# Cached attention for one token per sequence on one core: order of the last loads, and order of the tail on VectorE, TensorE and ScalarE

## The chip, the core and the metric

The kernel runs on one core of one Trainium2 chip. The core has TensorE (PE in the profile; PEld is its weight load), VectorE (DVE), ScalarE (ACT), GpSimd (POOL) and SyncE (SP), which here issues the loads. 16 DMA engines move the data. The metric is the device time of one execution in microseconds; the number compared is the median over several executions.

## What is computed

One decoding step of grouped attention over the last 512 positions of a cache: 32 sequences ("batches"), 32 query heads, 8 K/V heads, head size 128, all bf16.

```python
B, Sq, D = 32, 1, 512
Hq, Hkv, Sk, Dh = 32, 8, 2048, 128
W = min(4096, max(256, Sk // 4))                 # 512
q = (x @ wq).reshape(B, Sq, Hq, Dh).transpose(0, 2, 1, 3)
k = repeat(k_cache[:, :, Sk - W:, :], 4, axis=1)
v = repeat(v_cache[:, :, Sk - W:, :], 4, axis=1)
p = softmax(einsum("bhqd,bhkd->bhqk", q, k) * Dh ** -0.5)
o = einsum("bhqk,bhkd->bhqd", p, v)
out = o.transpose(0, 2, 1, 3).reshape(B, Sq, Hq * Dh) @ wo
```

K and V of the window are 32 MB each (in units of 1024 KB), `wq` and `wo` 4 MB each.

## The kernel before

Each engine has a program of its own, written out by hand; engines meet at semaphores. Nothing reorders the instructions of an engine: what stands first runs first, and a wait holds back all that is behind it on that engine.

The work goes by quads, four batches each, eight in all. K comes in 16 chunks of 2 MB, two for a quad. Three K buffers rotate, so chunk n may be issued only when chunk n-3 has been transposed (the wait on `pe_T[3]` in `load_k`). V comes by batch, two transfers of 0.5 MB for each, into eight rotating buffers: batch b may be issued only when batch b-8 has been multiplied (the wait on `pe_PV` in `load_v`). All these loads stand in one order on SP: chunk n, then the V of batches 2n-4 and 2n-3; after the last chunk the four remaining batches; then `wo` in eight pieces, into two of the K buffers; at the very end the store of the result.

A step v of the main loop (32 steps, four to a quad) does on TensorE:

- `transposes(v)`: half a K chunk, 32 blocks of 128x128, into four PSUM banks (`KT_ps`). DVE empties three of these (line 366), ACT the fourth (line 455).
- at the first step of a quad, `scores` of the quad before (line 258), into `S_ps`
- `pv_matmuls(v - 7)`: V of one batch times the transposed probabilities `PT_sb`, 32 matmuls (line 291), into `QO_ps`. This bank is single: batch b waits until DVE has copied batch b-1 out (`ot_evac`, line 403).
- at the third step of a quad, `pt_transposes` of the quad before (line 273): P, expanded by DVE to `P_ex`, is transposed into `PT_ps`, and ACT copies it to `PT_sb` in two halves (`pt_evac`, line 474). The batches of that quad wait for both halves.

Between scores and P transposes lies the softmax of a quad: DVE takes the maximum (372) and scales it (374), ACT takes the exponential (463), DVE the reciprocal (380), and four instructions of DVE, `p_expand`, write the probabilities into `P_ex` (389), one for each 32 partitions.

After the loop comes the tail: scores of the last quad, batches 25 to 27, P transposes of the last quad, `select` for batches 0 to 27 (line 303: 16 matmuls with the 0/1 matrix `band`, which arrange the heads for the output product; they write the two first banks of `KT_ps`, and DVE and ACT copy one half each to `o_sel`, lines 429 and 489), batches 28 to 31, `select` for these (303, copied at 433), the product with `wo` (340), copies (436, 496) and the store (167).

In the tail of before DVE runs: maximum, scaling, reciprocal, four expansions, then the copies of batches 25, 26, 27, the copy of the selection, and the copies of batches 28 to 31. ACT runs: exponential, the two halves of `pt_evac`, its half of the selection, and at the end its half of the output.

Of the kernel before, what the change touches and what calls it, by code (L numbers as in the profile page):

```python
# [12 lines left out]
def bass_standalone__sliding_block_cached__sampling_kernel(  # L13
# [7 lines left out]
):  # L21
    B, Sq, D = x.shape
    _, HKV, SK, DH = k_cache.shape
    HD = wq.shape[1]
    HQ = HD // DH
# [14 lines left out]
    NQUAD = B // 4  # L40
    NVB = 4 * NQUAD
    PVLAG = 7
    NCH = 2 * NQUAD
# [5 lines left out]
    SELCUT = 28  # L49

    with ExitStack() as es:
# [75 lines left out]
        def cache_rows(cache, b, h):  # L127
            return cache[b, 4 * h:4 * h + 4, SK - W:, :].rearrange("g (s r) d -> s g (r d)", s=NS)

        @block.sync  # L130
        def _(sp):
            for kt in range(1, DKT):
                sp.dma_start(wq_sb[:, kt, :], wq[kt * P:(kt + 1) * P, :]).then_inc(sem_wq[kt], 16)  # L133

            def load_k(n):
                q, e = divmod(n, 2)
                if n >= NK:
                    sp.wait_ge(pe_T[3], 2 * (n - NK) + 2)
                rows = k_cache[4 * q:4 * q + 4, :, SK - W:, :].rearrange("b g (s r) d -> (b g) s (r d)", s=KS)
                sp.dma_start(  # L140
                    K_sb[:, n % NK].rearrange("p r d -> p (r d)"), rows[:, :, e * CR * DH:(e + 1) * CR * DH]
                ).then_inc(sem_k[n % NK], 16)

            def load_v(b):
                if b >= NV:
                    sp.wait_ge(pe_PV, b - NV + 1)
                for h in range(2):
                    sp.dma_start(  # L148
                        V_sb[:, b % NV, h].rearrange("p r d -> p (r d)"), cache_rows(v_cache, b, h)
                    ).then_inc(sem_v[b % NV], 16)  # L150

            for n in range(NCH):
                load_k(n)
                if n >= 2:
                    load_v(2 * n - 4)
                    load_v(2 * n - 3)
            for b in range(B - 4, B):
                load_v(b)
            for hg in range(NHG):
                sp.wait_ge(pe_T[3], NVB - 4 + 2 * (hg // 4))  # L160
                sp.dma_start(
                    wo_sb[:, hg].rearrange("p i n -> p (i n)"),
                    wo[hg * 512:(hg + 1) * 512, :].rearrange("(m i) n -> m (i n)", i=4),
                ).then_inc(sem_wo[hg], 16)
            sp.wait_ge(dve_out, 2)
            sp.wait_ge(act_out, 2)
            sp.dma_start(
                out.rearrange("b s n -> b (s n)"), out_sb[:, :, :].rearrange("b c n -> b (c n)")
            ).then_inc(sem_out, 16)
            sp.wait_ge(sem_out, 16)  # L170
# [35 lines left out]
        def _(pe):  # L206
# [59 lines left out]
            def pt_transposes(q):  # L266
                pe.wait_ge(dve_P, 4 * q + 4)
                pe.wait_ge(act_PT, 2 * q)
                if q == 0:
                    pe.wait_ge(dve_qt, 1)  # L270
                    pe.wait_ge(act_qt, 1)
                for r in range(NR):
                    ins = pe.matmul(  # L273
                        PT_ps[:, r // 8, (r % 8) * 128:(r % 8 + 1) * 128],
                        lhsT=P_ex[:, r, :, :].rearrange("p s g -> p (s g)"),
                        rhs=ident[:, :],
                        start=True, stop=True, is_transpose=True, tile_position=(0, 0),
                    )
                    if r % 8 == 7:
                        ins.then_inc(pe_PT, 1)  # L280
# [39 lines left out]
            scores(NQUAD - 1)  # L320
            for b in range(NVB - PVLAG, SELCUT):
                pv_matmuls(b)
            pt_transposes(NQUAD - 1)
            pe.wait_ge(pool_band, 2)
            pe.wait_ge(dve_T, 3 * NVB)
            pe.wait_ge(act_T, NVB)
            nb = SELCUT
            select(0, nb, lambda i: KT_ps[:, i // 2, :].bitcast(F32)[
                :, (i % 2) * NHG * nb:(i % 2 + 1) * NHG * nb])
            for b in range(SELCUT, B):  # L330
                pv_matmuls(b)
            nl = B - SELCUT
# [16 lines left out]
        @block.vector  # L349
        def _(dve):  # L350
            dve.wait_ge(pe_xT, 1)
            dve.tensor_copy(
                xT_sb[:, :, :], S_ps[:, 0:DKT * 32].rearrange("p (kt b) -> p kt b", b=32)
            ).then_inc(dve_xT, 1)
            dve.wait_ge(pe_qt, 1)
            dve.tensor_copy(
                QT_sb[:, 0:16, :].rearrange("p h b -> p (h b)"), PT_ps[:, 0, :].bitcast(F32)
            ).then_inc(dve_qt, 1)

            def kt_evac(v, t):  # L360
                q = v // 4
                if v % 4 == 0 and t == 0 and q >= 2:
                    dve.wait_ge(pe_S, q - 1)
                dve.wait_ge(pe_T[t], v + 1)
                r0 = 32 * (v % 4) + 8 * t
                dve.tensor_copy(  # L366
                    KT[q % 2][:, r0:r0 + 8].rearrange("p r a s -> p (r a s)"), KT_ps[:, t, :]
                ).then_inc(dve_T, 1)

            def softmax_a(q):  # L370
                dve.wait_ge(pe_S, q + 1)
                dve.tensor_reduce(maxv[:, q:q + 1], S_ps[:, :], AX.X, ALU.max).then_inc(dve_sm, 1)  # L372
                dve.wait_ge(dve_sm, 2 * q + 1)
                dve.tensor_scalar(  # L374
                    negmax[:, q:q + 1], maxv[:, q:q + 1], -SCALE, None, op0=ALU.mult
                ).then_inc(dve_sm, 1)

            def softmax_b(q):
                dve.wait_ge(act_exp, q + 1)
                dve.reciprocal(recip[:, q:q + 1], sums[:, q:q + 1]).then_inc(dve_sm2, 1)  # L380
                dve.wait_ge(dve_sm2, q + 1)
                if q == 0:
                    dve.wait_ge(pool_ex, 1)
                else:
                    dve.wait_ge(pe_PT, 2 * q)

            def p_expand(q, c):
                rows = slice(32 * c, 32 * c + 32)
                dve.tensor_scalar(  # L389
                    P_ex[rows, :, :, c], P_f32[rows, :].rearrange("p (r s) -> p r s", r=NR),  # L390
                    recip[rows, q:q + 1], None, op0=ALU.mult,
                ).then_inc(dve_P, 1)

            def sel_evac(bank, i0, ni, b0, b1):
                return (
                    o_sel[:, i0:i0 + ni, :, b0:b1],
                    KT_ps[:, bank, :].bitcast(F32)[:, 0:ni * NHG * (b1 - b0)].rearrange(
                        "p (i g b) -> p i g b", i=ni, g=NHG),
                )

            def ot_evac(b):
                dve.wait_ge(pe_PV, b + 1)
                dve.tensor_copy(oT_sb[:, :, b], QO_ps[:, 0:HQ]).then_inc(dve_oT, 1)  # L403

            for v in range(NVB):
                q, k = divmod(v, 4)
                kt_evac(v, 0)
                if k == 1 and q >= 1:
                    softmax_b(q - 1)
                    p_expand(q - 1, 0)  # L410
                kt_evac(v, 1)
                if k == 1 and q >= 1:
                    p_expand(q - 1, 1)
                kt_evac(v, 2)
                if k == 1 and q >= 1:
                    p_expand(q - 1, 2)
                    p_expand(q - 1, 3)
                if k == 0 and q >= 1:
                    softmax_a(q - 1)
                if v >= PVLAG:  # L420
                    ot_evac(v - PVLAG)
            softmax_a(NQUAD - 1)
            softmax_b(NQUAD - 1)
            for c in range(G4):
                p_expand(NQUAD - 1, c)
            for b in range(NVB - PVLAG, SELCUT):
                ot_evac(b)
            dve.wait_ge(pe_sel, 1)
            dve.tensor_copy(*sel_evac(0, 0, 2, 0, SELCUT)).then_inc(dve_sel, 1)
            for b in range(SELCUT, B):  # L430
                ot_evac(b)
            dve.wait_ge(pe_sel, 2)
            dve.tensor_copy(*sel_evac(3, 0, 4, SELCUT, B)).then_inc(dve_sel, 1)
            dve.wait_ge(pe_fin, 1)
            for c in range(2):
                dve.tensor_copy(
                    out_sb[:, c, :], KT_ps[32 * c:32 * (c + 1), 2, :].bitcast(F32)[:, 0:128]
                ).then_inc(dve_out, 1)

        @block.scalar  # L440
        def _(act):
# [37 lines left out]
            for v in range(NVB):  # L479
# [4 lines left out]
                if k == 2 and q >= 1:  # L484
                    pt_evac(q - 1)
            do_exp(NQUAD - 1)
            pt_evac(NQUAD - 1)
            act.wait_ge(pe_sel, 1)
            act.activation(
                o_sel[:, 2:4, :, 0:SELCUT],  # L490
                KT_ps[:, 1, :].bitcast(F32)[:, 0:2 * NHG * SELCUT].rearrange("p (i g b) -> p i g b", i=2, g=NHG),
                ACTF.Copy,
            ).then_inc(act_sel, 1)
            act.wait_ge(pe_fin, 1)
            for c in range(2, 4):
                act.activation(
# [30 lines left out]
```

## Time and profile before

| what | value |
|---|---|
| median of 8 runs | 198.55 us (197.2 to 198.89) |
| the profiled execution | 197.96 us |
| its span | 196.2 us |
| PE busy | 139.6 us (71%) |
| DVE busy | 104.6 us (53%) |
| ACT busy | 57.5 us (29%) |
| mean granted TensorE clock | 0.896 |
| DMA | 75.95 MB, mean 387 GB/s |
| K chunk, issue to landing | 22.2 us (median) |
| V transfer, issue to landing | 20.6 us (median) |

The span runs from the first to the last instruction of the profiled execution. In a row of the timeline the first number is the start in microseconds, the second the length, then engine, line, operation, tile written and tile read, shape, and xcount, the number of instructions merged into the row. A bracket at the end tells how long the engine stood idle before and what released it. "SPq" rows are issues of transfers, not their landing. Where pipelined instructions overlap, a row can begin a little before the end of the one above.

### The profile page before, as it was taken

To read this page: it belongs to the slowest core of one execution; us is meant where nothing else is said; L and a number is where in the kernel's file an instruction comes from. 1 tells how busy PE (TensorE), PEld (TensorE's weight loads), DVE (VectorE), ACT (ScalarE), POOL (GpSimd) and SP (SyncE) were. 2 spreads that over 40 slices of the span, in tenths; PEclk is the share of its full clock that TensorE was granted. 3 is DMA by queue.
4 is the path that set the end of the run, shared out by engine and by line. 5 is a ranking of instruction groups with operands and counts; after the bars stand their busy time and mean duration, and the time that the engine had idled before them with its cause. 6 is when DMAs were issued, how large, how long until landed. Compare 5 with 4: busy or idle time off the path is not lost.

```text
span 196.2 us, 5984 instructions
## 1 busy us (share of the span) xinstructions
PE 139.6 (71%) x2724; PEld 119.1 (61%) x2724; DVE 104.6 (53%) x190; ACT 57.5 (29%) x70; POOL 11.9 (6%) x43
## 2 busy tenths in 40 slices
PE   0440989395896689677949598849884988808874
PEld 0330976294776667665749568745874588507774
DVE  0000694964469535963595349833983398472211
ACT  3000262315132622362115223522352234311301
POOL 8302000100010001000100010000000000000000
PEclk9999999969699969997888879997999699995857
DMA  5999999999999999999999999999999999999600
GB/s 202 426 451 421 428 398 440 395 427 410 435 400 430 405 419 419 413 421 412 412 413 432 408 431 407 423 413 423 403 421 413 425 402 406 407 410 406 255 17 7
DMA packets 13369, 75.95 MB, mean 387 GB/s; under 512 B 1504, under 2 KB 1568, under 8 KB 10784
## 3 DMA queue, kind: packets, MB, share of 16 engines
q1 hardware_dynamic: 13296, 75.54, 93.8%
q8 instruction: 21, 0.34, 0.7%
q10 hardware_dynamic: 48, 0.03, 0.1%
q14 instruction: 4, 0.03, 0.0%
HBM read 75.53 MB, written 0.03 MB: 385 GB/s over the span
## 4 chain that ended last, share of the span: by engine, by line
DMA 43%; PE 27%; SPq 14%; DVE 11%; issue 2%; ACT 1%; DVEq 0%
DMA K_sb<-in_k_cache_dram 43%; SPq L148 12%; PE KT_ps L241 11%; DVE P_ex L389 6%; PE QO_ps L291 6%; PE S_ps L258 6%; DVE w_sb L366 2%; PE KT_ps L340 2%; PE KT_ps L303 2%; DVE oT_sb L403 1%; PE PT_ps L273 1%; SPq L133 1%; SPq L140 1%; ACT w_sb L455 1%; ACT P_f L463 0%
## 5 line engine op out<-in xcount | busy, mean ns | idle before, releaser
L241 PE MATMUL KT_ps<-ident,K_sb 128*128 128x128 bf16 x1024 | 72.5, 238 | 31.7 <-DMA K_sb<-in_k_cache_dram 31.7
L241 PEld LDWEIGHTS KT_ps<-ident,K_sb 128*128 128x128 bf16 x1024 | 67.0, 107 | 34.1 <-DMA K_sb<-in_k_cache_dram 33.3
L366 DVE COPY KT_sb<-KT_ps 128x1024 bf16<-128x1024 bf16 x48 | 31.3, 688 | 18.9 <-PE KT_ps L241 18.6
L366 DVE COPY w_sb<-KT_ps 128x1024 bf16<-128x1024 bf16 x48 | 31.4, 688 | 14.9 <-PE KT_ps L241 14.7
L291 PE MATMUL QO_ps<-PT_sb,V_sb 128*128 128x16 bf16 x1024 | 30.9, 171 | 11.0 <-DVE oT_sb L403 10.7
L291 PEld LDWEIGHTS QO_ps<-PT_sb,V_sb 128*128 128x128 bf16 x1024 | 28.4, 97 | 16.5 <-DVE oT_sb L403 12.1
L455 ACT ACTIVATE KT_sb<-KT_ps 128x1024 bf16<-128x1024 bf16 x16 | 16.4, 1024 | 41.3 <-PE KT_ps L241 41.3
L455 ACT ACTIVATE w_sb<-KT_ps 128x1024 bf16<-128x1024 bf16 x16 | 16.4, 1025 | 35.5 <-PE KT_ps L241 35.5
L389 DVE TENSOR_SCALAR P_ex<-P_f,recip 32x512 bf16<-32x512 f32 x32 | 25.3, 792 | 1.3 <-DVE recip L380 0.3
L474 ACT ACTIVATE PT_sb<-PT_ps 128x1024 bf16<-128x1024 bf16 x16 | 15.5, 1021 | 14.3 <-PE PT_ps L273 14.3
L372 DVE TENSOR_REDUCE maxv<-S_ps 128x1 f32<-128x512 f32 x8 | 5.5, 691 | 21.8 <-PE S_ps L258 21.8
L403 DVE CAST oT_sb<-QO_ps 128x32 bf16<-128x32 f32 x32 | 9.5, 296 | 9.0 <-PE QO_ps L291 8.8
L203 POOL COPY QBD<-QT_sb 128x32 bf16<-128x32 bf16 x32 | 6.0, 232 | 124.8 <-PE S_ps L258 116.4
L463 ACT ACTIVATE P_f<-S_ps,negmax 128x512 f32<-128x512 f32 x8 | 5.5, 687 | 22.0 <-DVE negmax L374 22.0
L258 PE MATMUL S_ps<-w_sb,QBD 128*32 128x512 bf16 x128 | 11.2, 504 | 0.5 <-ACT w_sb L455 0.5
L258 PE MATMUL S_ps<-KT_sb,QBD 128*32 128x512 bf16 x128 | 11.2, 502 | 0.0
L273 PE MATMUL PT_ps<-ident,P_ex 128*128 128x128 bf16 x128 | 9.3, 232 | 0.0
L221 PE MATMUL PT_ps<-xT_sb,w_sb 128*128 128x32 bf16 x128 | 4.1, 188 | 6.4 <-DMA w_sb<-in_wq_dram 6.4
L273 PEld LDWEIGHTS PT_ps<-ident,P_ex 128*128 128x128 bf16 x128 | 8.1, 104 | 0.0
L221 PEld LDWEIGHTS PT_ps<-xT_sb,w_sb 128*128 128x128 bf16 x128 | 3.7, 104 | 6.8 <-DMA w_sb<-in_wq_dram 4.6
L258 PEld LDWEIGHTS S_ps<-w_sb,QBD 128*32 128x32 bf16 x128 | 3.7, 113 | 6.2 <-issue 6.2
L258 PEld LDWEIGHTS S_ps<-KT_sb,QBD 128*32 128x32 bf16 x128 | 3.6, 113 | 5.7 <-issue 5.6
(30 smaller groups left out, 29.3 us busy)
## 6 DMA issues: line engine op xcount, KB each, us to landing
K_sb<-in_k_cache_dram SPq DMA_DIRECT2D x16, 2048.0 KB, 22.2
V_sb<-in_v_cache_dram SPq DMA_DIRECT2D x64, 512.0 KB, 20.6
w_sb<-in_wq_dram SPq DMA_DIRECT2D x4, 1024.0 KB, 8.2
K_sb<-in_wo_dram SPq DMA_DIRECT2D x8, 512.0 KB, 15.0
x_sb<-in_x_dram ACTq DMA_DIRECT2D x1, 32.0 KB, 2.7
out_dram<-out_sb SPq DMA_DIRECT2D x1, 32.0 KB, 1.5
```

Source lines behind the costliest of these rows:

```text
L148: sp.dma_start(V_sb[:, b % NV, h].rearrange("p r d -> p (r d)"), cache_rows(v_cache, b, h)).then_inc(sem_v[b % NV], 16)
L203: pool.tensor_copy(dst, src).then_inc(pool_qbd, 1)
L221: ins = pe.matmul(PT_ps[:, h // 16, :].bitcast(F32)[:, (h % 16) * 32:(h % 16 + 1) * 32], lhsT=wq_sb[:, kt, h * DH:(h + 1) * DH], rhs=xT_sb ...
L241: ins = pe.matmul(KT_ps[:, t, i * 128:(i + 1) * 128], lhsT=K_sb[:, n % NK, 32 * (v % 2) + 8 * t + i, :], rhs=ident[:, :], start=True, stop ...
L258: ins = pe.matmul(S_ps[32 * c:32 * c + 32, :], lhsT=QBD[:, (4 * q + j) % NQB, g, :], rhs=KT[q % 2][:, :, G * j + g, :], start=(j == 0 and ...
L273: ins = pe.matmul(PT_ps[:, r // 8, (r % 8) * 128:(r % 8 + 1) * 128], lhsT=P_ex[:, r, :, :].rearrange("p s g -> p (s g)"), rhs=ident[:, :], ...
L291: ins = pe.matmul(QO_ps[:, 16 * h:16 * h + 16], lhsT=V_sb[:, b % NV, h, r, :], rhs=PT_sb[:, q % 2, r, :].rearrange("p (c n) -> p c n", c=G ...
L366: dve.tensor_copy(KT[q % 2][:, r0:r0 + 8].rearrange("p r a s -> p (r a s)"), KT_ps[:, t, :]).then_inc(dve_T, 1)
L389: dve.tensor_scalar(P_ex[rows, :, :, c], P_f32[rows, :].rearrange("p (r s) -> p r s", r=NR), recip[rows, q:q + 1], None, op0=ALU.mult,).th ...
L403: dve.tensor_copy(oT_sb[:, :, b], QO_ps[:, 0:HQ]).then_inc(dve_oT, 1)
L455: act.activation(KT[q % 2][:, r0:r0 + 8].rearrange("p r a s -> p (r a s)"), KT_ps[:, 3, :], ACTF.Copy).then_inc(act_T, 1)
L474: act.activation(PT_sb[:, q % 2, 8 * i:8 * i + 8, :].rearrange("p r n -> p (r n)"), PT_ps[:, i, :], ACTF.Copy,).then_inc(act_PT, 1)
```

## The change

In the loads, the V batches that stood between K chunks 14 and 15 (24 and 25) and those that stood after chunk 15 (26 and 27) are all issued after chunk 15, ahead of 28 to 31. In the tail, DVE copies batch 25 out before the reciprocal and the copies of 26 and 27 between the expansions; TensorE does the selection of batches 0 to 27 before the last P transposes; and ACT copies its half of the selection before the two halves of `PT_sb`. The instructions are the same in kind and number.

```diff
             for n in range(NCH):
                 load_k(n)
-                if n >= 2:
+                if 2 <= n < NCH - 2:
                     load_v(2 * n - 4)
                     load_v(2 * n - 3)
-            for b in range(B - 4, B):
+            for b in range(B - 8, B):
                 load_v(b)
...
             scores(NQUAD - 1)
             for b in range(NVB - PVLAG, SELCUT):
                 pv_matmuls(b)
-            pt_transposes(NQUAD - 1)
             pe.wait_ge(pool_band, 2)
             pe.wait_ge(dve_T, 3 * NVB)
             pe.wait_ge(act_T, NVB)
             nb = SELCUT
             select(0, nb, lambda i: KT_ps[:, i // 2, :].bitcast(F32)[
                 :, (i % 2) * NHG * nb:(i % 2 + 1) * NHG * nb])
+            pt_transposes(NQUAD - 1)
             for b in range(SELCUT, B):
                 pv_matmuls(b)
...
             softmax_a(NQUAD - 1)
+            ot_evac(NVB - PVLAG)
             softmax_b(NQUAD - 1)
             for c in range(G4):
                 p_expand(NQUAD - 1, c)
-            for b in range(NVB - PVLAG, SELCUT):
-                ot_evac(b)
+                if NVB - PVLAG + 1 + c < SELCUT:
+                    ot_evac(NVB - PVLAG + 1 + c)
             dve.wait_ge(pe_sel, 1)
...
             do_exp(NQUAD - 1)
-            pt_evac(NQUAD - 1)
             act.wait_ge(pe_sel, 1)
             act.activation(
                 o_sel[:, 2:4, :, 0:SELCUT],
...
             ).then_inc(act_sel, 1)
+            pt_evac(NQUAD - 1)
             act.wait_ge(pe_fin, 1)
```

With `NVB = 32`, `PVLAG = 7`, `SELCUT = 28`, `NCH = 16` and `B = 32`, the loops above cover batches 25 to 27 before the cut and 28 to 31 after it.

## Prediction, made before the changed kernel had run

> **What bounds the kernel now.** I read the busy slices first, then the chain of waits, then the timeline of the last quads, then the granted clock by microsecond. The page says that transfers run without a pause almost to the end:
>
> ```profile
> DMA  5999999999999999999999999999999999999600
> DMA 43%; PE 27%; SPq 14%; DVE 11%; issue 2%; ACT 1%; DVEq 0%
> ```
>
> The second line is the chain that ended last, by engine. Up to the last quad it consists of K chunks and the queue that issues them; no compute engine sets the pace there. The timeline around the last two K chunks shows when they are issued (SPq), and what each issue stands behind:
>
> ```profile
> 128.88 1.02 SPq L140 DMA_DIRECT2D K_sb<-in_k_cache_dram  x1
> 129.94 9.01 SPq L148 DMA_DIRECT2D V_sb<-in_v_cache_dram  x4
> ...
> 137.59 1.95 PE L241 MATMUL KT_ps<-ident,K_sb 128*128 128x128 bf16 x32
> ...
> 139.57 0.54 SPq L140 DMA_DIRECT2D K_sb<-in_k_cache_dram  x1
> ```
>
> K chunk 14 goes out at 128.88 us, the four V transfers of batches 24 and 25 after it, chunk 15 at 139.57. Chunk 15 needs the buffer of chunk 12, which is free when the transposes of v=25 end: 137.59 + 1.95 = 139.54 us. So its issue is gated by TensorE, not by the V issues ahead of it. It lands 21.5 us later, where the next view shows PE waiting for it:
>
> ```profile
> 161.07 1.96 PE L241 MATMUL KT_ps<-ident,K_sb 128*128 128x128 bf16 x32 [0.84 <-DMA K_sb<-in_k_cache_dram]
> ...
> 163.47 0.30 DVE L403 CAST oT_sb<-QO_ps 128x32 bf16<-128x32 f32 x1
> 163.58 1.89 DVE L366 COPY w_sb<-KT_ps 128x1024 bf16<-128x1024 bf16 x3
> ...
> 163.82 0.96 PE L291 MATMUL QO_ps<-PT_sb,V_sb 128*128 128x16 bf16 x32 [0.79 <-DVE oT_sb L403]
> ```
>
> PE stood 0.84 us for chunk 15, transposed v=30, and then stood again, 0.79 us, for the evacuation of batch 22, which DVE reached only at 163.47 behind the four P expansions of quad 6. From the landing of chunk 14 (151.1) that DVE sequence is closed up. The tail, in the same timeline:
>
> ```profile
> 171.19 0.96 PE L291 MATMUL QO_ps<-PT_sb,V_sb 128*128 128x16 bf16 x32
> ...
> 172.02 0.15 DVE L374 TENSOR_SCALAR negmax<-maxv 128x1 f32<-128x1 f32 x1
> ...
> 173.47 3.24 DVE L389 TENSOR_SCALAR P_ex<-P_f,recip 32x512 bf16<-32x512 f32 x4 [0.29 <-DVE recip L380]
> 176.74 0.30 DVE L403 CAST oT_sb<-QO_ps 128x32 bf16<-128x32 f32 x1
> ...
> 177.10 1.02 PE L291 MATMUL QO_ps<-PT_sb,V_sb 128*128 128x16 bf16 x32 [4.95 <-DVE oT_sb L403]
> 178.16 0.30 DVE L403 CAST oT_sb<-QO_ps 128x32 bf16<-128x32 f32 x1 [1.12 <-PE QO_ps L291]
> ...
> 178.51 1.02 PE L291 MATMUL QO_ps<-PT_sb,V_sb 128*128 128x16 bf16 x32 [0.39 <-DVE oT_sb L403]
> ...
> 179.39 1.87 PE L273 MATMUL PT_ps<-ident,P_ex 128*128 128x128 bf16 x16
> ...
> 180.50 1.94 ACT L474 ACTIVATE PT_sb<-PT_ps 128x1024 bf16<-128x1024 bf16 x2 [7.51 <-PE PT_ps L273]
> ...
> 181.05 2.69 PE L303 MATMUL KT_ps<-oT_sb,band 128*128 128x224 bf16 x16
> ...
> 183.57 0.95 PE L291 MATMUL QO_ps<-PT_sb,V_sb 128*128 128x16 bf16 x32
> ```
>
> Batch 25 is multiplied by 172.15, but its evacuation waits until 176.74 behind softmax and four expansions; PE idles 4.95 us. Then batch 26, batch 27, the P transposes of quad 7, the selection and batch 28 follow each other. The clock and DMA share in single microseconds (PE busy, clock, DMA share, GB/s):
>
> ```profile
> 176.00:177.00 1.00, 0.00 (x0) 0.62 1.01 401
> 183.00:184.00 1.00, 1.00 (x24) 0.96 0.63 254
> 187.00:188.00 1.00, 0.61 (x23) 0.50 0.03 12
> ```
>
> The clock is half from about 176.25 (0.62 is the mean of 0.24 us full and 0.76 us half) to 183.07, and the last output weights land between 187 and 188 us.
>
> **Part 1, the loads.** Nothing is added or removed: K chunk 15 passes four V issues, so in order of the queue 2 MB stand behind it instead of ahead of it. At the 410 GB/s of the rows around 170 us, 4 x 0.52 MB are 5.1 us: chunk 15 lands at about 156 instead of 161. What SP must pass on the way: it now stands at the wait for v=25 from 129.9 to 139.57, and the V transfers of batches 24 and 25 go out from about 140 on, 10 us later than before. Behind them are V26 to V28, whose buffers are free by 148.4, and 11 issues between 139.57 and 149 at 0.54 to 0.7 us each (the shortest and the median V issue) take 6 to 8 us, so V29 (free at 157.6) and the output weights go out as before. This queue's transfers land about in the order of issue (chunks 14 and 15 went out 10.7 us apart and landed 10.0 apart), so batches 24 and 25 land at 161, where chunk 15 did; PE needs batch 24 at 167.34. Covered by 6 us; without that cover each us late would cost a us.
>
> The gain of Part 1 I take as zero. With chunk 15 there, v=30's transposes start at 160.25, when PE finishes batch 22, and end at 162.2 instead of 163.0. Next in PE's order is batch 23, and it waits for the cast at 163.47, which no part of this edit moves: 163.82 as before. The 0.84 us go into the second stall, 0.79 becoming about 1.6. Ends for the range: 0.84 us gained if that stall shrank too, and a loss taken up under the rivals.
>
> **Part 2, the casts among the expansions.** The same three casts of 0.30 us, placed earlier. Cast 25 at 172.20 (negmax ends 172.17; batch 25 is done) ends 172.50, ahead of the reciprocal at 173.02, which waits for the exponential anyway: free. PE starts batch 26 at 172.55 (a cast's end to the next matmul is 0.05 to 0.06) and ends at 173.55. Expansion 0 runs 173.47 to 174.25; cast 26 from 174.28 to 174.58; batch 27 from 174.63 to 175.6. Expansion 1 ends 175.4; cast 27 waits 0.25 for batch 27 and runs 175.63 to 175.95; expansions 2 and 3 end at 177.55, against 176.71. So the expansions end 0.84 us later and the casts of 25 to 27 are all out by 175.95 instead of 179.87.
>
> **Part 3, the selection ahead of the P transposes.** The selection starts at 176.0. In the trace it takes 2.52 us from its start to that of batch 28: 2.02 at half clock and 0.50 at full, so all at half clock 3.02 and all at full 1.51. I take the row as it is, as the clock's step can fall on either side. The P transposes start at 178.54 (expansions done at 177.55, no wait). From their start to ACT's first copy were 1.11 us, two copies 1.94: PT is ready at 181.59, batch 28 starts at 181.64. Before, PT was ready at 182.44, but PE was in the selection until 183.57: there the selection covered ACT's copies, and now nothing does. Between 181.64 and 183.57 lies the gain: **1.93 us**. ACT's selection copy (0.54) and DVE's (0.62) start at about 178.7 and end before the first PT half; they cost nothing. From batch 28 on every instruction is as before, 12.6 us to the end. The output weights are landed at 187.5 while the first is needed at 188.1 and the last at 191.2.
>
> Sum: 0 + 1.93 against a profiled execution of 197.96 us (span 196.2 and 1.8 around it), so 196.0 there. The median of the eight runs is 0.6 higher, 198.55: **196.6 us**.
>
> The trace shows the clock falling after 4 us of idle PE and rising after the closed-up transposes and selection. [...] By the page alone the selection could be anything from 1.5 to 3.0 us, the sum 195.3 to 197.1.
>
> **Rivals.**
> - *Full clock in the tail.* The stall of 4.95 us, in which the clock fell, is gone. Selection 1.51 (ends 177.5), transposes from 177.6, first copy 0.70 later as in quad 6 (164.64 weight load to 165.34 copy), copies 1.94: batch 28 at 180.3, gain 3.28, **195.3**. Against: batches 28 to 30, with the same pauses, ran from 183.07 at full clock and lost it again at 186.5.
> - *Chunk 15 counts.* The 0.84 us of its wait come on top: **195.8**. Against: the second stall, and the chain, which passes through chunk 14 and the expansions.
> - *Clock falls one step sooner.* Half clock from 169 on: scores 3.18 us (as at 153.58) instead of 2.46, two batches 0.06 each, selection 3.02: 1.43 - 0.72 - 0.12 = 0.6 gained, **198.0**, no change. For it: scores did run so at 153.58; against: here PE is busy up to the scores.
> - *The queue runs thin (slower).* SP issues nothing for 9.6 us. If the transfers lost all of that, the last output weights would land at 197.1 instead of 191.2 where they are needed: 5.9 lost less 1.93 gained, **202.5**. Up to 3.7 us lost costs nothing; from 5.6 on the kernel is slower. Against: at 139.57 chunk 14 still has 11.5 us to land, so there is work queued throughout.
> - That Part 1 doesn't do what it says is in my forecast: issue time the same, landing 5 us sooner, nothing for the end.
>
> **How the numbers follow.** Forecast 0.60, full clock 0.12, chunk 15 0.08, clock sooner 0.12, queue 0.08. 0.5% is 1.0 us, about what a measurement of this kernel can tell from no change. Faster: 0.57 of the forecast (a small part of it may fall short of 1.0) + 0.12 + 0.08 = 0.77; same 0.12 + 0.03 = 0.15; slower 0.08. The forecast's own bounds (selection 3.02 to 1.51) are 197.1 to 195.3; taking in most of the clock case, the range is 195.2 to 197.9.
>
> **What would show it.** SP issues chunk 15 at about 139.6 and batch 24 after it; v=30's transposes no longer wait for K, and batch 23's wait for the cast grows to about 1.6 us. Four separate expansions with casts between, ending near 177.55; selection from 176.0, transposes about 178.5, batch 28 about 181.6 behind ACT. Wrong if the DMA share sinks between 140 and 160, if batch 24 waits for V, if batch 23 starts before 163.5, or if the selection is done at full clock.

## The result, and the profile after

The changed kernel ran in 195.80 us (median of 19 runs, 194.79 to 196.82), the kernel before in 198.04 us (median of 54). The ratio is 0.9897, 95% interval 0.9877 to 0.9916: faster by 1.0%, some 2.0 us. The span of the profiled execution went from 196.2 to 194.4 us. The ratios leave out runs more than 1.5% above the fastest of their kernel and the medians take all, so where the runs of one kernel spread over 3 us or more, as several do below, the two can differ by half a per cent.

The page of the changed kernel: busy share of the DMA engines in 40 slices, and the chain that ended last.

```profile
DMA  5999999999999999999999999999999999999820
DMA 44%; PE 27%; SPq 13%; DVE 10%; ACT 2%; issue 2%; DVEq 0%
```

The DMA engines are still busy for nine tenths or more of every slice from the second to the 37th (to 179.8 us), though SP issues nothing for ten microseconds. ACT's share of the chain rises from 1% to 2%: its two copies of PT are no longer covered. The timeline of the changed kernel (start, length, engine, line, what, and in brackets the idle time before it with its releaser):

```profile
128.83 11.30 SPq L140 DMA_DIRECT2D K_sb<-in_k_cache_dram  x2
...
137.62 1.95 PE L241 MATMUL KT_ps<-ident,K_sb 128*128 128x128 bf16 x32
...
140.18 26.06 SPq L148 DMA_DIRECT2D V_sb<-in_v_cache_dram  x16
...
151.18 3.13 PE L241 MATMUL KT_ps<-ident,K_sb 128*128 128x128 bf16 x32 [2.76 <-DMA K_sb<-in_k_cache_dram]
...
154.24 2.76 PE L258 MATMUL S_ps<-KT_sb,QBD 128*32 128x512 bf16 x32
...
160.33 1.05 PE L241 MATMUL KT_ps<-ident,K_sb 128*128 128x128 bf16 x16
...
162.09 1.07 PE L241 MATMUL KT_ps<-ident,K_sb 128*128 128x128 bf16 x16 [0.70 <-DVE w_sb L366]
...
163.71 0.30 DVE L403 CAST oT_sb<-QO_ps 128x32 bf16<-128x32 f32 x1
...
164.06 0.96 PE L291 MATMUL QO_ps<-PT_sb,V_sb 128*128 128x16 bf16 x32 [0.91 <-DVE oT_sb L403]
...
169.03 2.47 PE L258 MATMUL S_ps<-w_sb,QBD 128*32 128x512 bf16 x32 [0.50 <-ACT w_sb L456]
...
172.43 0.30 DVE L403 CAST oT_sb<-QO_ps 128x32 bf16<-128x32 f32 x1
...
173.47 0.78 DVE L389 TENSOR_SCALAR P_ex<-P_f,recip 32x512 bf16<-32x512 f32 x1
174.06 0.33 DVE L403 CAST oT_sb<-QO_ps 128x32 bf16<-128x32 f32 x1
...
175.44 0.30 DVE L403 CAST oT_sb<-QO_ps 128x32 bf16<-128x32 f32 x1 [0.23 <-PE QO_ps L291]
175.77 1.62 DVE L389 TENSOR_SCALAR P_ex<-P_f,recip 32x512 bf16<-32x512 f32 x2
...
175.88 3.15 PE L303 MATMUL KT_ps<-oT_sb,band 128*128 128x224 bf16 x16 [0.48 <-DVE oT_sb L403]
...
178.82 1.17 PE L273 MATMUL PT_ps<-ident,P_ex 128*128 128x128 bf16 x16
...
179.64 1.94 ACT L475 ACTIVATE PT_sb<-PT_ps 128x1024 bf16<-128x1024 bf16 x2
181.63 0.96 PE L291 MATMUL QO_ps<-PT_sb,V_sb 128*128 128x16 bf16 x32 [1.64 <-ACT PT_sb L475]
```

Chunk 15 is issued when v=25 is transposed (137.62 + 1.95 = 139.57; the first SPq row ends at 140.13), and V from 140.18 on. TensorE no longer waits for K at v=30: it stands at other places instead, 0.70 us until DVE has emptied a bank and 0.91 us for the cast of batch 22. In the tail the casts stand between the expansions, the selection runs from 175.88, and batch 28 starts at 181.63.

Rows of the kernel before, for comparison here and below:

```profile
151.13 2.52 PE L241 MATMUL KT_ps<-ident,K_sb 128*128 128x128 bf16 x32 [2.74 <-DMA K_sb<-in_k_cache_dram]
...
153.58 3.18 PE L258 MATMUL S_ps<-KT_sb,QBD 128*32 128x512 bf16 x32
...
156.80 0.69 DVE L372 TENSOR_REDUCE maxv<-S_ps 128x1 f32<-128x512 f32 x1 [3.06 <-PE S_ps L258]
...
161.09 0.69 DVE L366 COPY w_sb<-KT_ps 128x1024 bf16<-128x1024 bf16 x1
...
168.79 2.46 PE L258 MATMUL S_ps<-w_sb,QBD 128*32 128x512 bf16 x32 [0.50 <-ACT w_sb L455]
```

A measure that is free of waits further up is the stretch from the start of the last scores to batch 28: before 183.57 - 168.79 = 14.78 us, after 181.63 - 169.03 = 12.60, so 2.18 us gained. The scores themselves start 0.24 us later than before (17.85 us after chunk 14 is there instead of 17.66, and chunk 14 itself 0.05 later), and from batch 28 to the end of the span it is 12.77 instead of 12.63 us: 2.18 - 0.24 - 0.14 = 1.80, the difference of the two spans. The measure still moves by some tenths from one execution to the next: among the runs below, e1, with the tail of before, has 14.30 us, and e2, e5, e6, e9, e10 and e11, with the tail of the change, have 12.27 to 12.52. The selection in it took 2.62 us in e9, 2.90 in e10 and 3.15 in the changed kernel, there at half clock (0.50 from 176 to 179 us).

### The profile page after: what moved, and what is told of

It reads as the page before. It is cut to its first block, busy times and chain, and to the rows that moved or that the text cites. A ratio compares the mean times of both kernels' runs of the same rounds, so it can differ in the third digit from the quotient of the medians.

```text
span 194.4 us, 5984 instructions
## 1 busy us (share of the span) xinstructions
PE 141.4 (73%) x2724; PEld 121.9 (63%) x2724; DVE 104.9 (54%) x190; ACT 57.5 (30%) x70; POOL 11.9 (6%) x43
## 4 chain that ended last, share of the span: by engine, by line
DMA 44%; PE 27%; SPq 13%; DVE 10%; ACT 2%; issue 2%; DVEq 0%
DMA K_sb<-in_k_cache_dram 44%; PE KT_ps L241 12%; SPq L148 12%; PE QO_ps L291 5%; DVE P_ex L389 5%; PE S_ps L258 5%; DVE w_sb L366 2%; PE KT_ps L303 2%; PE KT_ps L340 2%; DVE oT_sb L403 1%; ACT PT_sb L475 1%; SPq L140 1%; SPq L133 1%; ACT w_sb L456 1%; PE PT_ps L273 0%
## 5 line engine op out<-in xcount | busy, mean ns | idle before, releaser
L241 PE MATMUL KT_ps<-ident,K_sb 128*128 128x128 bf16 x1024 | 76.2, 244 | 30.0 <-DMA K_sb<-in_k_cache_dram 29.2
L241 PEld LDWEIGHTS KT_ps<-ident,K_sb 128*128 128x128 bf16 x1024 | 71.0, 111 | 32.4 <-DMA K_sb<-in_k_cache_dram 30.5
L366 DVE COPY KT_sb<-KT_ps 128x1024 bf16<-128x1024 bf16 x48 | 31.8, 689 | 20.2 <-PE KT_ps L241 19.9
L366 DVE COPY w_sb<-KT_ps 128x1024 bf16<-128x1024 bf16 x48 | 31.6, 688 | 14.8 <-PE KT_ps L241 14.5
L475 ACT ACTIVATE PT_sb<-PT_ps 128x1024 bf16<-128x1024 bf16 x16 | 15.5, 1021 | 7.0 <-PE PT_ps L273 6.9
L258 PE MATMUL S_ps<-w_sb,QBD 128*32 128x512 bf16 x128 | 10.3, 469 | 0.5 <-ACT w_sb L456 0.5
L258 PE MATMUL S_ps<-KT_sb,QBD 128*32 128x512 bf16 x128 | 10.2, 464 | 0.0
L273 PE MATMUL PT_ps<-ident,P_ex 128*128 128x128 bf16 x128 | 8.6, 220 | 0.0
L273 PEld LDWEIGHTS PT_ps<-ident,P_ex 128*128 128x128 bf16 x128 | 7.5, 99 | 0.1
```

Source lines behind the costliest of these rows:

```text
L241: ins = pe.matmul(KT_ps[:, t, i * 128:(i + 1) * 128], lhsT=K_sb[:, n % NK, 32 * (v % 2) + 8 * t + i, :], rhs=ident[:, :], start=True, stop ...
L258: ins = pe.matmul(S_ps[32 * c:32 * c + 32, :], lhsT=QBD[:, (4 * q + j) % NQB, g, :], rhs=KT[q % 2][:, :, G * j + g, :], start=(j == 0 and ...
L273: ins = pe.matmul(PT_ps[:, r // 8, (r % 8) * 128:(r % 8 + 1) * 128], lhsT=P_ex[:, r, :, :].rearrange("p s g -> p (s g)"), rhs=ident[:, :], ...
L366: dve.tensor_copy(KT[q % 2][:, r0:r0 + 8].rearrange("p r a s -> p (r a s)"), KT_ps[:, t, :]).then_inc(dve_T, 1)
L475: act.activation(PT_sb[:, q % 2, 8 * i:8 * i + 8, :].rearrange("p r n -> p (r n)"), PT_ps[:, i, :], ACTF.Copy,).then_inc(act_PT, 1)
```

## Experiments

Theory: the whole gain is the tail's; the order of the loads gives nothing, as the wait it removes was covered. Rivals: chunk 15 counts; the queue runs thin; and within the tail, that the swap of selection and P transposes and not the casts brings the gain.

### The parts one by one

**The loads alone** (e1): the two lines of the load order, the tail as before.

> The loads of the change alone, tail as before. Theory (the wait for chunk 15 was hidden behind the second stall): v=30's transposes start without a wait for K at about 160.3 us, batch 23 starts at the same distance from batch 22 as before, scores of the last quad to batch 28 stay at 14.8 us, time ratio to before 1.000 (within 0.002). Rival 'chunk 15 counts': 0.84 us less, ratio 0.996. Rival 'the queue runs thin': DMA share sinks between 140 and 150 us, ratio above 1.005.

Measured: 198.59 us against 198.69, ratio 0.9976 (0.9919 to 1.0032): no difference that this can tell, as the interval holds both the theory's 1.000 and the rival's 0.996. The trace holds something that the theory didn't expect, which is read below beside e2.

**The tail alone** (e2): the edits on TensorE, VectorE and ScalarE, the load order as before.

> The tail of the change alone, loads as before. Theory: all of the gain, scores of the last quad to batch 28 in 12.6 us instead of 14.8, ratio 0.990. Rival 'chunk 15 counts': a part of the gain is missing, ratio 0.994.

Measured: 196.44 us against 198.69, ratio 0.9944 (0.9908 to 0.9980); scores to batch 28 in 183.83 - 171.31 = 12.52 us. The tail's own stretch is as expected. The time is not: the ratio is the rival's 0.994, and the theory's 0.990 lies just outside the interval. But the two medians differ by 2.25 us, as much as those of the whole change, twice what the ratio shows: the time alone decides neither way.

**The casts alone** (e3):

```diff
             softmax_a(NQUAD - 1)
+            ot_evac(NVB - PVLAG)
             softmax_b(NQUAD - 1)
             for c in range(G4):
                 p_expand(NQUAD - 1, c)
-            for b in range(NVB - PVLAG, SELCUT):
-                ot_evac(b)
+                if NVB - PVLAG + 1 + c < SELCUT:
+                    ot_evac(NVB - PVLAG + 1 + c)
```

> Only the three casts among the expansions; selection behind the P transposes as before, loads as before. Theory (the casts brought nearly all, the swap of selection and transposes little): P transposes start when the expansions end (8.8 us after the scores), selection 1.7 us later, batch 28 after it, 13.0 us after the scores: gain 1.8 us, ratio 0.991. Rival (the selection ahead of the transposes is what fills the pause): batch 28 stays 14.8 us after the scores, ratio 1.000.

Measured: 196.49 us, ratio 0.9925 (0.9892 to 0.9957). The timeline of this run, with the scores at 169.05:

```profile
177.48 1.89 PE L273 MATMUL PT_ps<-ident,P_ex 128*128 128x128 bf16 x16 [2.03 <-DVE P_ex L389]
178.61 1.94 ACT L475 ACTIVATE PT_sb<-PT_ps 128x1024 bf16<-128x1024 bf16 x2 [5.36 <-PE PT_ps L273]
179.16 2.90 PE L303 MATMUL KT_ps<-oT_sb,band 128*128 128x224 bf16 x16
181.90 0.95 PE L291 MATMUL QO_ps<-PT_sb,V_sb 128*128 128x16 bf16 x32
```

Batch 28 starts 181.90 - 169.05 = 12.85 us after the scores. So of the 2.18 us, 1.93 come with the casts alone, by these traces. The P transposes now wait 2.03 us for the expansions, but the selection behind them covers ScalarE's copies (178.61 to 180.55) again.

**The selection alone** (e4), on TensorE; ScalarE's copies are reordered as in the change, which is not shown again here:

```diff
-            pt_transposes(NQUAD - 1)
             pe.wait_ge(pool_band, 2)
...
             select(0, nb, lambda i: KT_ps[:, i // 2, :].bitcast(F32)[
                 :, (i % 2) * NHG * nb:(i % 2 + 1) * NHG * nb])
+            pt_transposes(NQUAD - 1)
```

> Only the selection ahead of the P transposes (on TensorE and ScalarE); casts behind the four expansions and loads as before. Theory: selection at 179.9 us, P transposes behind it at 182.4 or later, ScalarE's copies no longer covered, batch 28 about 16.5 to 17.2 us after the scores instead of 14.8: slower by 1.8 to 2.4 us, ratio 1.009 to 1.012. Rival (the swap helps by itself): ratio 0.995 or below.

Measured: 200.38 us, ratio 1.0150 (1.0097 to 1.0203): slower, somewhat more than expected.

```profile
180.36 3.15 PE L303 MATMUL KT_ps<-oT_sb,band 128*128 128x224 bf16 x16 [0.48 <-DVE oT_sb L403]
183.29 1.91 PE L273 MATMUL PT_ps<-ident,P_ex 128*128 128x128 bf16 x16
...
184.45 1.94 ACT L474 ACTIVATE PT_sb<-PT_ps 128x1024 bf16<-128x1024 bf16 x2 [0.37 <-PE PT_ps L273]
186.45 0.96 PE L291 MATMUL QO_ps<-PT_sb,V_sb 128*128 128x16 bf16 x32 [1.24 <-ACT PT_sb L474]
```

With scores at 169.14 it is 17.31 us to batch 28, 2.53 more than before. The swap by itself does harm, because nothing covers the copies of PT any more: TensorE waits 1.24 us for them. With the casts it is worth 12.85 - 12.60 = 0.25 us in these two traces, which is within the 0.33 us by which executions with the tail of the change differ (12.27 to 12.60). Nearly all of the tail's gain belongs to three casts of 0.3 us.

### What the order of the loads is worth

e1 and e2 differ in the loads, and in both profiled executions TensorE's granted clock was full from 151 to 156 us (1.00 in every microsecond), other than in those of the kernels before (0.50 from 153 to 155) and after (0.50 from 152 to 155). First the loads of the change (e1), then those of before (e2): v=28, the scores of quad 6, v=30, the scores of quad 7.

```profile
150.84 1.96 PE L241 MATMUL KT_ps<-ident,K_sb 128*128 128x128 bf16 x32 [1.84 <-DMA K_sb<-in_k_cache_dram]
152.74 2.47 PE L258 MATMUL S_ps<-KT_sb,QBD 128*32 128x512 bf16 x32
...
158.54 1.05 PE L241 MATMUL KT_ps<-ident,K_sb 128*128 128x128 bf16 x16
...
167.25 2.46 PE L258 MATMUL S_ps<-w_sb,QBD 128*32 128x512 bf16 x32 [0.50 <-ACT w_sb L455]
```

```profile
151.01 1.96 PE L241 MATMUL KT_ps<-ident,K_sb 128*128 128x128 bf16 x32 [1.78 <-DMA K_sb<-in_k_cache_dram]
152.90 2.47 PE L258 MATMUL S_ps<-KT_sb,QBD 128*32 128x512 bf16 x32
...
162.56 3.60 PE L241 MATMUL KT_ps<-ident,K_sb 128*128 128x128 bf16 x32 [3.71 <-DMA K_sb<-in_k_cache_dram]
...
171.31 2.46 PE L258 MATMUL S_ps<-w_sb,QBD 128*32 128x512 bf16 x32 [0.50 <-ACT w_sb L456]
```

The clock of e2 in single microseconds (PE busy, clock, DMA share, GB/s), in the wait ahead of its third row:

```profile
159.00:160.00 1.00, 0.00 (x0) 1.00 1.10 455
...
161.00:162.00 1.00, 0.00 (x0) 0.50 1.00 389
```

From the landing of chunk 14 (first row) to the last scores it is 16.41 us in e1 and 20.30 in e2. TensorE is ready for v=30 7.70 and 7.84 us after chunk 14, some 1.3 us sooner than in the kernel before (9.11). With the new order chunk 15 is there. With the old one TensorE waits 3.71 us, its clock falls to half in that wait, and v=30 takes 3.60 us instead of 1.96. Of the 3.71 us, 0.84 stood in the kernel before too, 1.27 are the earlier arrival, and 1.6 are chunk 15's, which came 11.55 us after chunk 14 instead of 9.94: v=24 had taken 3.59 us instead of 2.92, as long as v=30 at half clock, so the buffer came free later and chunk 15 was issued at 140.42 instead of 139.57, which is the larger part of the 1.6.

These two are the extremes of their kernels: e1's profiled execution was the fastest of its twelve (195.70 us, median 198.59), e2's the slowest of its twelve (198.44, median 196.44). The 3.9 us are the difference of two unusual executions, not of two kernels.

In the kernels before and after the same stretch was 17.66 and 17.85 us, and in e3 and e4, with the old loads, 17.88 and 17.94 (e3 had a clock of 0.50 from 151 to 154 us; v=28 took 3.44 us in e3 and 3.49 in e4). With the new loads it is 16.42 in e8 below, at full clock as in e1 (1.00 from 151 to 156 us), and 18.84 in e7, where v=28 and its scores took 3.60 and 3.27 us instead of e8's 1.96 and 2.47 (clock 0.5 in the slice of the page from 150.7 to 155.6). So in these traces the order is worth nothing where v=28 and its scores run partly at half clock, and 3.9 us where they run at full clock. The theory falls for the second kind.

Two pairs were to show that with times.

**Keeping the clock up** (e5 with the loads of the change, e6 with those of before, both with the new tail). Ahead of the first chunk of a quad, from the third quad on (`NWARM` is 40):

```diff
+                    if t == 0 and v % 4 == 0 and v >= 8:
+                        pe.wait_ge(act_exp, v // 4 - 1)
+                        for _i in range(NWARM):
+                            pe.matmul(
+                                S_ps[:, 0:128], lhsT=ident[:, :], rhs=ident[:, :],
+                                start=True, stop=True, tile_position=(0, 0), skip_group_check=True,
+                            )
```

> The changed kernel, with 40 matmuls of the identity into the score bank ahead of the first K chunk of each quad from the third on, so that TensorE's clock doesn't fall while it waits there. Question: what the order of the loads is worth when the quad of chunk 14 runs at full clock. Theory now (hidden at half clock, not hidden at full clock): half v=28 and its scores take 4.4 us instead of 5.7, v=30 finds chunk 15 landed and doesn't wait, scores of the last quad start at about 167.3 us instead of 169.0; time 194.5 to 195, ratio to before 0.983. Rival (the loads never matter): same time as the run with the loads of before.

> The same matmuls of the identity with the tail of the change but the loads of before. Theory: TensorE reaches v=30 at about 158.7 us, chunk 15 lands at 161 to 162.5, a wait of 2.4 us or more stands there again, scores of the last quad start at 169 to 171: 1.5 to 2.5 us slower than the run with the changed loads, ratio to before 0.990 to 0.994. Rival (the loads never matter): scores at 167.3 here too and the same time.

Measured: e5 196.31 us, ratio 0.9886 (0.9840 to 0.9932); e6 197.70 us, ratio 0.9976 (0.9949 to 1.0002). The pair lies 1.4 us apart in the direction expected, but e5 is slower than the 194.5 to 195 us expected, and the means failed: the clock was not held. The timeline of e5, with the 40 matmuls in the first row:

```profile
147.17 2.39 PE L237 MATMUL S_ps<-ident 128*128 128x128 bf16 x40
...
152.23 2.42 PE L249 MATMUL KT_ps<-ident,K_sb 128*128 128x128 bf16 x32 [2.67 <-DMA K_sb<-in_k_cache_dram]
```

The matmuls were through 2.67 us before chunk 14 landed, the clock fell at about 153.6 (0.78 in the microsecond from 153, 0.50 in the two after it), and the scores behind v=28 again took 3.24 us. In these two executions the stretch from chunk 14 to the last scores is 17.63 and 17.65 us, the same for both load orders, which is the case of half clock once more (0.50 from 154 to 156 in e5 and to 157 in e6). e6's was among the fastest two of its twelve (196.66 us). The difference in time must come from other executions and is not explained by these traces.

**Less work ahead of v=30** (e9 with the loads of the change, e10 with those of before, both with the new tail). In the scores of quad 6 only one of the four batches is computed, so these two kernels leave out a part of the attention (the other three batches get flat weights):

```diff
-                for j in range(4):
+                nj = 1 if q == NQUAD - 2 else 4
+                for j in range(nj):
...
-                            start=(j == 0 and h == 0), stop=(j == 3 and h == 1), tile_position=(0, 32 * c),
+                            start=(j == 0 and h == 0), stop=(j == nj - 1 and h == 1), tile_position=(0, 32 * c),
```

> The changed kernel, with three quarters of the scores of quad 6 left out (24 of 32 matmuls; batches 25 to 27 get flat weights there), which brings TensorE to v=30 about 1.9 us sooner at full clock and 2.4 at half, whatever the clock does. Theory (the order of the loads pays as soon as TensorE is early): the scores of the last quad start 1.9 to 2.4 us sooner after chunk 14 lands, 14.5 to 15.5 us after it, no wait for chunk 15; time 1.5 to 2.4 us below the changed kernel, about 193.5 to 194.3. Rival (the loads never matter): the saving is the same with the loads of before.

> The same quarter of scores, tail of the change, loads of before. Theory: TensorE waits 2.5 to 3.5 us for chunk 15, which lands about 10 us after chunk 14 as before; scores of the last quad 17 us or more after chunk 14 lands, 1.2 us or more slower than with the changed loads, and more (up to 4 us) if the clock falls in that wait. Rival (the loads never matter): no wait, the time of the other run.

Measured: e9 193.94 us, ratio 0.9781 (0.9732 to 0.9830); e10 196.45 us, ratio 0.9906 (0.9867 to 0.9945). The intervals don't meet; the two are 2.5 us apart. e9, then e10:

```profile
150.98 3.41 PE L241 MATMUL KT_ps<-ident,K_sb 128*128 128x128 bf16 x32 [2.39 <-DMA K_sb<-in_k_cache_dram]
...
160.16 1.07 PE L241 MATMUL KT_ps<-ident,K_sb 128*128 128x128 bf16 x16 [0.71 <-DVE w_sb L367]
...
167.11 2.47 PE L259 MATMUL S_ps<-w_sb,QBD 128*32 128x512 bf16 x32 [0.50 <-ACT w_sb L457]
```

```profile
151.21 3.54 PE L241 MATMUL KT_ps<-ident,K_sb 128*128 128x128 bf16 x32 [2.19 <-DMA K_sb<-in_k_cache_dram]
...
161.15 3.26 PE L241 MATMUL KT_ps<-ident,K_sb 128*128 128x128 bf16 x32 [2.25 <-DMA K_sb<-in_k_cache_dram]
...
169.25 2.45 PE L259 MATMUL S_ps<-w_sb,QBD 128*32 128x512 bf16 x32 [0.50 <-ACT w_sb L457]
```

Both had half clock at v=28 (0.50 from 151 to 154 us in e9, from 152 to 154 in e10). With the new loads the work left out arrives at the last scores (16.13 us after chunk 14 instead of 17.85; 14.5 to 15.5 was expected, too much, as v=28 itself took 3.41 us). With the old loads it ends in a wait of 2.25 us for chunk 15, behind which the clock falls to half (1.00 in the microsecond from 160, 0.78 and 0.50 in the next two; v=30 takes 3.26 us; it took 2.08 in e3), and the stretch is 18.04 us, longer than with all scores. Of the 2.5 us between the two kernels 1.91 stand in this stretch; most of the rest is the output product (2.97 us in e9, 3.60 in e10), which the order of the loads doesn't touch. Here TensorE is early by less work and not by its clock: it is ready for v=30 7.43 and 7.70 us after chunk 14 instead of 9.11, some 1.5 us early, and the place of chunk 15 in the queue decides; a clock that falls in the wait (e2) or behind it (e10) adds to the price.

**Chunk 15 still later** (e11): behind the V of batches 24 to 27.

```diff
             for n in range(NCH):
+                if n == NCH - 1:
+                    for b in range(B - 8, B - 4):
+                        load_v(b)
                 load_k(n)
...
-            for b in range(B - 8, B):
+            for b in range(B - 4, B):
                 load_v(b)
```

> The changed kernel with chunk 15 put the other way, behind the V of batches 24 to 27 (4 MB ahead of it instead of none). Theory: it lands at about 166 us, TensorE waits some 5 us for it, scores of the last quad at 173 to 175 us instead of 169.0, time 4 to 6 us above the changed kernel, 200 to 202. Rival (the expansions hide its wait): less than 1 us above the changed kernel.

Measured: 203.2 us, ratio 1.0242 (1.0193 to 1.0292), some 7 us above the changed kernel and more than expected.

```profile
167.63 3.59 PE L244 MATMUL KT_ps<-ident,K_sb 128*128 128x128 bf16 x32 [7.08 <-DMA K_sb<-in_k_cache_dram]
...
176.14 2.48 PE L261 MATMUL S_ps<-w_sb,QBD 128*32 128x512 bf16 x32 [0.50 <-ACT w_sb L459]
```

Chunk 15 is there at 167.63 instead of 161.07, v=30 waits 7.08 us for it and takes 3.59, and the last scores start at 176.14. About five microseconds sooner than before (an estimate of the prediction; no trace shows that landing) can be worth nothing, and 6.6 later cost seven: the wait of 0.84 us in the old profile was the edge of a slope.

### A version that beats both

Two kernels go on from the changed one. In e7 the P transposes come first again, VectorE copies the second half of PT while ScalarE copies the first, and the selection is cut in four pieces:

```diff
+            pt_transposes(NQUAD - 1)
...
-            select(0, nb, lambda i: KT_ps[:, i // 2, :].bitcast(F32)[
-                :, (i % 2) * NHG * nb:(i % 2 + 1) * NHG * nb])
-            pt_transposes(NQUAD - 1)
             for b in range(SELCUT, B):
                 pv_matmuls(b)
+                select(0, nb, lambda i: KT_ps[:, i // 2, :].bitcast(F32)[
+                    :, (i % 2) * NHG * nb:(i % 2 + 1) * NHG * nb], [b - SELCUT])
```

> The changed kernel, but in the tail the P transposes come first, VectorE copies the second half of PT while ScalarE copies the first, and the selection of batches 0 to 27 is cut in four pieces of four matmuls, one behind each of the batches 28 to 31, where TensorE waits for the cast; ScalarE copies both its halves. Theory: batch 28 starts about 1.5 us sooner than in the changed kernel (11.1 us after the scores instead of 12.6), each piece costs 0.1 to 0.35 more than the pause it fills, so 0.3 to 1.1 us faster than the changed kernel. Rival (the selection in the pauses holds up the batches by its whole length of 2.5 to 3 us less the 1.5): 0 to 0.5 us slower than the changed kernel.

Measured: 195.21 us, ratio 0.9801 (0.9754 to 0.9848), about 0.6 us below the changed kernel by the medians, though its six runs spread over 3.8 us. In its trace batch 28 starts 181.37 - 169.99 = 11.38 us after the scores (11.1 expected). In e8 ScalarE also does two of the last four expansions:

```diff
+            for c in range(2, G4):
+                rows = slice(32 * c, 32 * c + 32)
+                act.activation(
+                    P_ex[rows, :, :, c], P_f32[rows, :].rearrange("p (r s) -> p r s", r=NR),
+                    ACTF.Copy, scale=recip[rows, NQUAD - 1:NQUAD],
+                ).then_inc(act_P, 1)
```

> The same tail, and ScalarE does two of the four last P expansions while VectorE does two. Theory: the expansions end about 2.3 us sooner, at 6.2 us after the scores instead of 8.5, P transposes start behind batch 27, batch 28 8 to 8.5 us after the scores instead of 12.6; the output product then waits for the last output weights, which land at about 187.5 us: gain over the changed kernel 3 to 4 us, 192 to 193. Rival (the transfers of the output weights end no sooner and every later step waits for them): 1.5 us or less.

Measured: 193.26 us, ratio 0.9754 (0.9714 to 0.9794): 2.5 us below the changed kernel by the medians, less than the 3 to 4 expected.

```profile
172.26 2.89 ACT L500 ACTIVATE P_ex<-P_f,recip 32x512 bf16<-32x512 f32 x2 [0.23 <-DVE recip L386]
...
175.24 1.87 PE L277 MATMUL PT_ps<-ident,P_ex 128*128 128x128 bf16 x16 [1.06 <-issue]
...
178.20 1.00 PE L297 MATMUL QO_ps<-PT_sb,V_sb 128*128 128x16 bf16 x32 [1.09 <-DVE PT_sb L436]
...
187.92 0.41 PE L346 MATMUL KT_ps<-K_sb,o_sel 128*32 128x128 bf16 x16 [0.65 <-DMA K_sb<-in_wo_dram]
```

ScalarE's two expansions took 2.89 us, nearly as long as VectorE's four (3.24 in the kernel before), so the P transposes start at 175.24 and batch 28 is 178.20 - 167.83 = 10.37 us behind the scores instead of 8 to 8.5. And the last output weights now end a wait of 0.65 us at 187.92: the tail has come up against the transfers. Of the 3.5 us between the spans of the changed kernel and of e8 (194.4 and 190.9), 2.23 are this shorter stretch; 1.43 stand ahead of the last scores, where this execution had v=28 at full clock (1.00; its chunk 14 came 0.23 later).

## Why the prediction was right, and where it was not

- *Size and sign.* 1.93 us were forecast and 196.6 us; measured about 2.0 and 195.8, inside the range. In the traces the tail gave 2.18 us. The sum held.
- *Part 2, the casts.* Cast 25 went ahead of the reciprocal at no cost, the casts were out by 175.74 (175.95 was said), the expansions ended at 177.39 (177.55). The prediction did not say which of Parts 2 and 3 carries the gain; e3 and e4 show that the casts alone bring 1.93 us and the swap alone loses 2.53 in their traces.
- *Part 3, the selection.* From its start to the P transposes took 2.94 us, near the bound of all half clock (3.02), not the 2.52 taken. Other terms made that up: with the clock rising at 179 (0.50 in the microsecond before, 0.98 in the one after), transposes to first copy took 0.82 us instead of 1.11, and the expansions began 0.25 us sooner after the reciprocal; on the other side the last scores started 0.24 us later. So batch 28 at 181.63 against 181.64 said is luck: four terms of a quarter to half a microsecond cancelled.
- *Part 1, the loads: "The gain of Part 1 I take as zero".* This is the step that failed in part. Issue at 139.57, the wait for K gone, and no gain in the profiled execution were right. Wrong was that v=30 would end at 162.2: it stopped half-way for a bank (0.70 us) and ended at 163.16, so batch 23's wait for the cast was 0.91 us and not 1.6. The bank could be seen in the profile of before, where VectorE's last copy of v=29 runs until 161.78. Wrong above all was to take one profiled execution for all. The prediction called VectorE's sequence closed up from the landing of chunk 14 on, but in that profile VectorE stands 3.06 us in it, until 156.80, for scores that TensorE computes partly at half clock. So the second stall, which was to cover the first, hangs on that clock, as does TensorE's arrival at 160.25, hardly earlier than chunk 15. At full clock the old order cost 3.9 us more in that stretch (e2) than the new one (e1), in two extreme executions; with less work ahead of v=30 the new order is worth 1.9 us in the stretch and 2.5 us in time. The prediction weighed the clock in the tail, where it came to 0.3 to 0.4 us, and not here.
- *How much of the 2.0 us the loads are, stays open.* e1's ratio is 0.9976, with 0.6% either way; the medians of e2 and of the changed kernel lie equally far below before; the ratios of the changed kernel to e2 and of e5 to e6 say 0.5 and 0.9%. Three of the thirteen profiled executions had v=28 and its scores at full clock (e1, e2 and e8); how often that is in all runs was not counted. Three of e1's twelve runs took 195.7 to 196.3 us and nine 197.85 to 199.94, which would fit an order that pays in a few executions, but only the fastest has a trace.
- *Rivals.* The queue did not run thin: the DMA share stayed near 1.0 between 140 and 160 us (0.91 to 1.14 by microsecond). The full clock in the tail did not come; selection and batches 29 to 31 ran at half (0.50 from 176 to 179 and from 183 to 187 us). The clock did fall sooner than before, at 175.6 instead of 176.25 us, but behind the scores, which took 2.47 us at full clock. Chunk 15 did not count in the profiled execution, and does where TensorE is early (e2, e10).

## What to carry to other kernels

When an engine waits behind a block of its neighbour's instructions, look first for the short ones that free it: three copies of 0.3 us, moved between longer instructions, were worth more in this tail than the swap of its large steps (1.93 us against 0.25, or a loss of 2.53 without the casts). A wait that a second wait covers is free only at the pace of that execution; before its price is set to zero, work out how early the waiting engine could come at its fastest. And before a covering step is moved, name what it covered: the selection hid ScalarE's copies, and moved alone it made the kernel slower.

## What the runs showed of the hardware that was not expected

- With a cast ahead of the reciprocal an idle time of VectorE was gone. Without it VectorE stands 0.29 us between the reciprocal and the first expansion of the tail (before), with it the expansion follows within 0.04 us (after, e8, e9, e10). The cause was not tried.
- Two expansions of 32x512 elements from f32 to bf16 took 2.89 us on ScalarE; on VectorE one took 0.78 us and one 0.79 (e8).
- The clock fell behind an idle time of TensorE of 2.67 us (e5: idle from 149.56 to 152.23; 1.00 in the microsecond from 152, 0.78 in the next, 0.50 from 154 to 156); in the tail of before it fell after some 4 us (idle from 172.15, 0.62 in the microsecond from 176). Nor did the length of the idle time decide alone: the clock was 0.50 at the end of one of 2.39 us (e9, at 150.98) and still 1.00 at the end of one of 2.74 us (before, at 151.13).
